# Long convolution and SwiGLU block: even/odd decimated transforms, a folded filter, spectra kept by lane, and shift rows loaded in even partition groups

## The chip, the cores and the metric

The kernel runs on one core of a Trainium2 chip. Times are device microseconds (us) of whole executions. The kernel before takes 399.01 us (median of 4 runs, the profiled one among them, 397.53 to 400.22). "Span" is the length of the one execution that was profiled.

Engine names in the profiles: PE is TensorE (matrix products), PEld its weight load, DVE is VectorE, ACT is ScalarE, POOL is GpSimd, SP is SyncE, which only issues transfers here. "L379" is line 379 of that run's own kernel. The same statement has a slightly different number in different runs.

## The reference, cut to what matters

There are 2048 positions of 640 channels. A short causal filter (4 taps) is applied to `k`, the result is multiplied by `v`, and a causal convolution as long as the sequence follows. Then come a residual, a layer norm and a feed-forward with a gate.

```python
def _A_ref(q, k, v, shift_k, ssm_k, ssm_D):
    k_pad = jnp.pad(k, ((0, 0), (ks - 1, 0), (0, 0)))
    for t in range(ks):                                   # ks = 4
        k_shift = k_shift + k_pad[:, t:t + S, :] * shift_k[:, ks - 1 - t][None, None, :]
    kv = k_shift * v
    ...                                                   # y = causal convolution of kv with ssm_k, by FFT
    y = y + kv * ssm_D[None, None, :]
    return q * y

x = A_q
h = x + _A_ref(_layernorm(x), A_k, A_v, A_shift_k, A_ssm_k, A_ssm_D)
h2 = h + (_silu(_layernorm(h) @ w_gate) * (_layernorm(h) @ w_up)) @ w_down      # 640 -> 1728 -> 640
```

The comparison with the reference is weak on the convolution: the four experiments that spoil it on purpose (a1, a1b, a2, d1) are all recorded as "correct". That the result of the convolution is small beside `x` would explain it, but was not measured. "Correct" says little of the convolution.

## The kernel before

The sequence is cut into 4 blocks of 512 positions. Each block of `kv` is multiplied by a matrix of cosines and sines (`fwd_transform`), each piece of the filter likewise, the spectra are multiplied and added over earlier blocks (`cmac`), and one inverse transform a block gives the convolution. The parts that the change and the argument touch:

```python
    def fwd_transform(src4, dst8):                        # 8 x 4 x 2 matmuls of 320 columns
        for ct in range(NCT):
            ps = psA.tile([P, 2, 512], FP32, name="ps_mm")
            for kt in range(TT_PER_BLK):
                lhsT = WF_t[:, kt, ct * P:(ct + 1) * P]
                for h in range(2):
                    nc.tensor.matmul(ps[:, h, 0:NH], lhsT, src4[:, kt, h * NH:(h + 1) * NH],
                                     start=(kt == 0), stop=(kt == TT_PER_BLK - 1))
            nc.scalar.copy(r3(dst8[:, ct, :]), ps3(ps))

    def cmac(A, X, G, T, first):                          # complex product and sum: 8 operations of 2560
        ...
            nc.vector.tensor_mul(T, Xc, Gc)
            nc.vector.tensor_add(Ac, Ac, T)
            nc.vector.tensor_mul(T, Xs, Gs)
            nc.vector.tensor_sub(Ac, Ac, T)
            ...

    def conv_front_tiles(j, tiles, st):
            ...
            for jj in range(4):                           # k is loaded four times, shifted by a row
                kj = iop.tile([P, D], BF16, name=f"k{jj}")
                if ti == 0 and jj > 0:
                    nc.gpsimd.memset(kj[0:jj, :], 0.0)
                    nc.sync.dma_start(out=kj[jj:P, :], in_=kk[0:P - jj, :])
                else:
                    nc.sync.dma_start(out=kj[:], in_=kk[r0 - jj:r0 - jj + P, :])
            ...

    def ffn_quarter(q):
            ...
                nc.scalar.activation(sig[:csz, :], ps_g[:csz, :], ACT.Sigmoid)
                gc = ffio.tile([P, MBLK], BF16, name="gc")
                nc.scalar.copy(gc[:csz, :], ps_g[:csz, :])
                uc = ffio.tile([P, MBLK], BF16, name="uc")
                nc.scalar.copy(uc[:csz, :], ps_u[:csz, :])
                gs = ffio.tile([P, MBLK], BF16, name="gs")
                nc.vector.tensor_mul(gs[:csz, :], gc[:csz, :], sig[:csz, :])
                nc.vector.tensor_mul(tT[:csz, c, :], gs[:csz, :], uc[:csz, :])
        ...
    for k in range(1, NB):
        conv_front(k)
        pair(k - 1, 1)
        conv_back(k)
        ffn_quarter(k - 1)
        for pp in range(2, NB - (k - 1)):
            pair(k - 1, pp)
```

## Time and profile before

| | before |
|---|---|
| median of the runs | 399.01 us (4 runs, with the profiled one) |
| span of the profiled execution | 397.7 us |
| PE / DVE / ACT busy | 325.7 / 254.7 / 253.8 us |
| matmuls of 320 columns / of 512 columns in the program | 1216 / 560 |
| bytes moved | 68.91 MB |

The page of the kernel before: the span, busy time of each engine with its share and number of instructions, then the busy share in tenths of 40 equal slices, and the chain of work that ended last, by engine.

```profile
span 397.7 us, 5429 instructions
PE 325.7 (82%) x1914; PEld 185.3 (47%) x1936; DVE 254.7 (64%) x413; ACT 253.8 (64%) x447; POOL 68.1 (17%) x95
PE   1038874497899779999779899897998999999995
DVE  1185498500629989999949999983699723233321
DMA  8589847513886996366863716351043332254111
PE 33%; issue 25%; ACT 14%; DMA 13%; DVE 11%; SPq 2%; POOL 2%; POOLq 0%; DVEq 0%; ACTq 0%
```

A digit is about 10 us.

The three steps of a feed-forward chunk that one operation can replace, from the groups by line of the kernel before (columns: line, engine, operation, operands, shapes, count, busy us, mean ns of one, and the idle time before them):

```profile
L362 ACT CAST gc<-ps_g 128x512 bf16<-128x512 f32 x52 | 30.3, 583 | 0.0
L366 DVE TENSOR_TENSOR gs<-gc,sig 128x512 bf16<-128x512 bf16 x52 | 21.6, 419 | 27.6 <-ACT gc L362 27.6
```

### The profile page before, as it was taken

What the parts mean: (1) busy time and instruction counts of PE and PEld (TensorE: products, weight loads), DVE (VectorE), ACT (ScalarE), POOL (GpSimd) and SP (SyncE); (2) the same over time, 40 slices, a digit from 0 to 9 for tenths busy, and PEclk for the clock granted to TensorE, in tenths of its full rate; (3) what the DMA queues carried; (4) which work ended last, traced back from release to release, by engine and by line L of the source; (5) the groups of instructions that cost most, each with busy time, mean ns of one, the idle gap of its engine ahead of it and who ended that gap; (6) DMA issues with size and microseconds to landing.
All of it is one profiled execution on the core that took longest, in us unless ns stands there. A gap on an engine that the chain in (4) does not pass through costs nothing.

```text
span 397.7 us, 5429 instructions
## 1 busy us (share of the span) xinstructions
PE 325.7 (82%) x1914; PEld 185.3 (47%) x1936; DVE 254.7 (64%) x413; ACT 253.8 (64%) x447; POOL 68.1 (17%) x95
## 2 busy tenths in 40 slices
PE   1038874497899779999779899897998999999995
PEld 1025542364567324565354355454534554544463
DVE  1185498500629989999949999983699723233321
ACT  1259607999786636479987539976664697166610
POOL 5000001000000303203102211131131111433121
PEclk9999969589999969999999999989999999999999
DMA  8589847513886996366863716351043332254111
GB/s 249 180 314 357 296 146 242 157 66 109 321 303 259 356 335 218 101 178 220 305 190 101 266 49 199 104 155 56 16 141 106 112 96 77 100 155 142 52 51 49
DMA packets 33610, 68.91 MB, mean 173 GB/s; under 512 B 4213, under 2 KB 25904, under 8 KB 31920
## 3 DMA queue, kind: packets, MB, share of 16 engines
q1 hardware_dynamic: 26800, 45.63, 33.7%
q0 software_dynamic: 6784, 22.94, 18.5%
q8 instruction: 15, 0.25, 0.2%
q14 instruction: 11, 0.09, 0.1%
HBM read 56.77 MB, written 11.80 MB: 172 GB/s over the span
## 4 chain that ended last, share of the span: by engine, by line
PE 33%; issue 25%; ACT 14%; DMA 13%; DVE 11%; SPq 2%; POOL 2%; POOLq 0%; DVEq 0%; ACTq 0%
PE ps_g L356 11%; PE ps_mm L376 7%; PE ps_mm L153 6%; PE ps_u L358 6%; PE ps_mm L303 4%; DMA wu_g<-in_B_w_up_dram 3%; ACT gc L362 3%; ACT xln_blk L139 3%; DMA k_148<-in_A_k_dram 2%; DMA wg_g<-in_B_w_gate_dram 2%; ACT junk L124 2%; SPq L250 2%; ACT sig L360 2%; DMA WF_t<-const_wf 1%; DMA wbig<-in_A_shift_k_dram 1%
## 5 line engine op out<-in xcount | busy, mean ns | idle before, releaser
L356 PE MATMUL ps_g<-hlnT,wg_g 128*128 128x512 bf16 (+1 forms) x268 | 70.9, 386 | 11.1 <-DMA wg_g<-in_B_w_gate_dram 6.1
L153 PEld LDWEIGHTS <-WF_t 128*128 128x128 bf16 x512 | 51.3, 101 | 48.7 <-DMA WF_t<-const_wf 13.8
L358 PE MATMUL ps_u<-hlnT,wu_g 128*128 128x512 bf16 (+1 forms) x270 | 70.3, 384 | 2.0 <-ACT uc L364 1.3
L376 PE MATMUL ps_mm<-wd_sb,tT 128*128 128x320 bf16 x448 | 69.6, 302 | 1.0 <-DVE tT L367 1.0
L360 ACT ACTIVATE sig<-ps_g 128x512 bf16<-128x512 f32 (+1 forms) x56 | 33.4, 597 | 50.0 <-PE ps_g L356 44.5
L376 PEld LDWEIGHTS <-tT 128*128 128x128 bf16 x448 | 41.9, 98 | 25.6 <-issue 7.1
L346 POOL DMA_DIRECT2D wg_g<-in_B_w_gate_dram x28 | 24.4, 873 | 168.9 <-PE ps_g L356 156.2
L153 PE MATMUL ps_mm<-gT,WF_t 128*128 128x320 bf16 x256 | 40.8, 313 | 15.1 <-DMA WF_t<-const_wf 13.5
L356 PEld LDWEIGHTS <-wg_g 128*128 128x128 bf16 (+1 forms) x280 | 27.3, 99 | 47.4 <-issue 14.7
L153 PE MATMUL ps_mm<-kv_blk,WF_t 128*128 128x320 bf16 x256 | 39.0, 307 | 6.9 <-ACT Xcur L155 3.9
L358 PEld LDWEIGHTS <-wu_g 128*128 128x128 bf16 (+1 forms) x280 | 27.5, 99 | 34.6 <-issue 3.7
L366 DVE TENSOR_TENSOR gs<-gc,sig 128x512 bf16<-128x512 bf16 (+1 forms) x56 | 23.2, 419 | 30.3 <-ACT gc L362 30.3
L364 ACT CAST uc<-ps_u 128x512 bf16<-128x512 f32 (+1 forms) x56 | 32.8, 586 | 10.8 <-DVE tT L367 3.3
L303 PEld LDWEIGHTS <-WI_t 128*128 128x128 bf16 x256 | 25.8, 102 | 17.5 <-issue 5.3
L362 ACT CAST gc<-ps_g 128x512 bf16<-128x512 f32 (+1 forms) x56 | 32.6, 582 | 0.0
L348 POOL DMA_DIRECT2D wu_g<-in_B_w_up_dram x28 | 24.4, 871 | 34.1 <-PE ps_u L358 21.5
L367 DVE TENSOR_TENSOR tT<-gs,uc 128x512 bf16<-128x512 bf16 (+1 forms) x56 | 23.2, 419 | 7.3 <-ACT uc L364 7.0
L155 ACT CAST Xcur<-ps_mm 128x640 bf16<-128x640 f32 x32 | 21.7, 693 | 9.0 <-PE ps_mm L153 9.0
L124 ACT ACTIVATE junk<-h_t,zero_t 128x640 bf16<-128x640 bf16 x16 | 13.2, 828 | 21.8 <-DVE h_t L313 21.5
L261 DVE TENSOR_TENSOR kv_blk<-kv_blk,ktmp 128x640 bf16<-128x640 bf16 x48 | 23.4, 487 | 0.8
L124 ACT ACTIVATE junk<-x_t,zero_t 128x640 bf16<-128x640 bf16 x16 | 13.3, 831 | 13.0 <-DMA x_t<-in_A_q_dram 12.7
L382 POOL DMA_DIRECT2D out_dram<-o_t x16 | 8.8, 553 | 65.4 <-DVE o_t L381 52.0
(256 smaller groups left out, 412.7 us busy)
## 6 DMA issues: line engine op xcount, KB each, us to landing
wg_g<-in_B_w_gate_dram POOLq DMA_DIRECT2D x24, 320.0 KB, 3.6
wu_g<-in_B_w_up_dram POOLq DMA_DIRECT2D x24, 320.0 KB, 4.2
Hld_129<-hf_dram SPq DMA_DIRECT2D x3, 1280.0 KB, 5.5
Hld_130<-hf_dram SPq DMA_DIRECT2D x3, 1280.0 KB, 9.9
gst<-in_A_ssm_k_dram SPq DMA_DIRECT2D x4, 640.0 KB, 7.7
x_t<-in_A_q_dram SPq DMA_DIRECT2D x16, 160.0 KB, 5.4
v_t<-in_A_v_dram SPq DMA_DIRECT2D x16, 160.0 KB, 3.9
h_dram<-h_t SPq DMA_DIRECT2D x16, 160.0 KB, 2.7
```

Of the source, the lines that this page charges most:

```text
L124: nc.scalar.activation(junk[:], x_tile, ACT.Identity, bias=zero_t[:], scale=1.0, accum_out=mv_out[:, 0:1])
L153: nc.tensor.matmul(ps[:, h, 0:NH], lhsT, src4[:, kt, h * NH:(h + 1) * NH], start=(kt == 0), stop=(kt == TT_PER_BLK - 1))
L261: nc.vector.tensor_add(ks, ks, tmp[:])
L303: nc.tensor.matmul(ps[:, h, 0:NH], lhsT, Acc[:, ct, h * NH:(h + 1) * NH], start=(ct == 0), stop=(ct == NCT - 1))
L346: nc.gpsimd.dma_start(out=wg_g[:, :, 0:ncols], in_=B_w_gate[:, f0:f0 + ncols].rearrange("(kt p) f -> p kt f", p=P))
L348: nc.gpsimd.dma_start(out=wu_g[:, :, 0:ncols], in_=B_w_up[:, f0:f0 + ncols].rearrange("(kt p) f -> p kt f", p=P))
L356: nc.tensor.matmul(ps_g[:csz, :], wg_g[:, kt, off:off + csz], hlnT[:, kt, :], start=(kt == 0), stop=(kt == 4))
L358: nc.tensor.matmul(ps_u[:csz, :], wu_g[:, kt, off:off + csz], hlnT[:, kt, :], start=(kt == 0), stop=(kt == 4))
L360: nc.scalar.activation(sig[:csz, :], ps_g[:csz, :], ACT.Sigmoid)
L362: nc.scalar.copy(gc[:csz, :], ps_g[:csz, :])
L364: nc.scalar.copy(uc[:csz, :], ps_u[:csz, :])
L376: nc.tensor.matmul(ps_o[:, h, 0:NH], lhsT, wd_sb[:csz, c, h * NH:(h + 1) * NH], start=(c == 0), stop=(c == NFCH - 1))
```

## The change

The intent is to do less matrix work. The odd-frequency transform of 512 samples is split by the parity of the position (decimated), so that half of the products serve two frequencies. The filter is folded about its middle before its transform. Complex products become three real ones, on "lanes" S, D and E (sequences of 2 x 640 values a partition, S being made from the sum of D and E), two halves each. Spectra of earlier blocks and of the filter go to DRAM lane by lane and come back when they are needed. Positions are laid out so that partition p holds the four rows 4p to 4p+3, and one transfer of seven rows a partition gives all four taps. In block 0 partition 0 has no earlier rows, so 127 partitions are left to load. The last clause of the title is what the change does about them: it loads groups of 112, 8, 4, 2 and 1 partitions. SiLU is taken straight from PSUM. It is nearly a complete rewrite; the core of the diff, with cuts:

```diff
-    def fwd_transform(src4: bass.AP, dst8: bass.AP):
-        for ct in range(NCT):
-            ...
+    def x_transform(i, kv):
+        t = {}
+        for r in range(2):
+            for n in range(2):
+                dst = spt(f"x{n}{r}")
+                for c in range(2):
+                    ps = ps_mm()
+                    for a in range(2):
+                        s = 2 * a + r
+                        for h in range(2):
+                            nc.tensor.matmul(ps[:, h, 0:NH], cs_t[:, s, n, c * P:(c + 1) * P],
+                                             kv[:, s, h * NH:(h + 1) * NH], start=(a == 0), stop=(a == 1))
+                    evac(dst[:, c, :], ps, i == 0 and r == 1 and c == 1)
+                t[n, r] = dst
+        ...                                  # six sums and differences give lanes S, D, E
-                kj = iop.tile([P, D], BF16, name=f"k{jj}")
-                ...
+    def load_k(i):
+        kt = wk.tile([P, NS + 3, D], BF16, name="krun", bufs=1)
+        if i == 0:
+            nc.vector.memset(kt[0:1, 0:3, :], 0.0)
+            nc.scalar.dma_start(out=kt[0:1, 3:7, :], in_=kk[0:NS, :].rearrange("(o r) d -> o r d", o=1))
+            lo = P
+            while lo > 1:
+                hi, lo = lo, 16 if lo == P else lo // 2
+                (nc.sync if hi == P else nc.scalar).dma_start(
+                    out=flat(kt[lo:hi, :, :]),
+                    in_=bass.AP(tensor=kk.tensor, offset=kk.offset + (NS * lo - 3) * D, ap=[[NS * D, hi - lo], [1, 7 * D]]))
+        else:
+            nc.sync.dma_start(out=flat(kt[:]), in_=rows(kk, i, -3, 7))
+        return kt
...
+                for le in LANES:
+                    a = None
+                    for j in range(i):
+                        hl = load_lane(HD[i - j], le)
+                        xl = Xp[le] if j == i - 1 else load_lane(XD[j], le)
+                        nc.vector.tensor_mul(xl[:], xl[:], hl[:])
+                        if a is None:
+                            a = xl
+                        else:
+                            nc.vector.tensor_add(a[:], a[:], xl[:])
+                    acc[le] = a
...
+    def back(i, acc, xn):
+        ...                                  # inverse transform, h, its statistics
+        mean2, rs2 = ln_stats(h, (1, 3) if i == 0 else ())
+        hlnT = wk.tile([P, NDC, MBLK], BF16, name="hlnT", bufs=1)
+        hn = wkt("hn")
+        for a in range(2):
+            pt = psM.tile([P, 2, 1024], BF16, name="ps_tr", tag="ps_mm")
+            for r in range(2):
+                s = 2 * a + r
+                ln_apply(hn, h, mean2, rs2, s)
+                for kt in range(NDC):
+                    nc.tensor.transpose(pt[:, r, kt * P:(kt + 1) * P], hn[:, s, kt * P:(kt + 1) * P], ident[:])
+                nc.scalar.copy(...)
+        return h, hlnT
...
-                nc.scalar.activation(sig[:csz, :], ps_g[:csz, :], ACT.Sigmoid)
-                ...
+                    nc.scalar.activation(sg[0:np_, :], pss[0][0:np_, :], ACT.Silu)
+                    nc.scalar.copy(uc[0:np_, :], pss[-1][up_lo:up_lo + np_, :])
+                    nc.vector.tensor_mul(tT[0:np_, c, :], sg[0:np_, :], uc[0:np_, :])
...
+    for i in range(1, NB):
+        with at(CONV[i]):                    # at() sets the priority that orders each engine's queue
+            ...
+            nxt = back(i, acc, x_norm(i))
+        ffn(i - 1, *state)
+        state = nxt
```

## The prediction

> **What bounds the kernel now.** The page's first part gives PE 325.7 us (82%), DVE 254.7 (64%), ACT 253.8 (64%) of a 397.7 us span. By stage (busy time in 20 us windows) there are three regimes. To about 144 us the first block and the filter spectra are made; the chain of waits there passes through DMA (WF_t, 13.8 us of weight-load wait), PSUM evictions of ACT and transforms. From 120 to 260 us DVE is nearly full (18.9 to 19.7 of 20 us in most windows) as PE is, with interleaved feed-forward and convolution. From 320 us only the last feed-forward is left, on PE.
>
> **Costs, from groups kept apart by form.** A 320-column matmul costs 0.141 us in a dense run (56 in 7.92 us in the chain), a 512-column one 0.227 us (ten in 2.27 us). PSUM evictions on ACT take 0.69 us, statistics passes 0.83 and 0.74. A bf16 tensor_tensor takes 0.419 us for 512, 0.488 for 640, 1.482 for 2560 elements: 0.15 + 0.52 per thousand, so an estimated 0.82 for 1280. [...]
>
> **Removed.** 320-column matmuls fall from 1216 to 848, 512-column ones from 560 to 540: about 57 us of dense PE time (317 to 260). ACT loses one of three evictions in each feed-forward chunk, normalizations (32 x 0.91) and nearly all table loads (14 x 1.28), gains output evictions: about 206 us. The k rows are loaded once, not four times, q once.
>
> **Added.** The combinations of lanes on DVE: butterflies before and after, three real products for each complex one (6 of 1280 instead of 4 of 2560), folds. My count of the new instructions gives 267 us, slightly more than now. Spilled spectra: about 78 lane transfers of 0.33 MB; total bytes an estimated 62 MB (now 68.9).
>
> **On the critical path.** The new kernel becomes DVE-bound in the middle. My stage sum: block 0 ready by about 70 us; three filter pieces, bound by evictions, to 100-108 us (feed-forward starts here, now 144); then DVE works without much pause from the filter combination to the last inverse's inputs: 180 us of work, 190 with gaps between instructions, so to about 290. PE has slack there, waiting for lane products and for second-norm statistics before the transposes (8-13 us each, they stand ahead of the down projection). Then inverse, statistics, transposes (20 us), a dense down projection (16), last feed-forward (31 + 16), store (5): about 375 us. Overlaps that I count as serial pull it down a little: 368. So only about half of the PE saving arrives.
>
> **Predicted:** 368 us, 8 in 10 between 340 and 393. Chances: faster 0.86, same 0.11, slower 0.03.
>
> **What would show it.** PE busy near 265-285 us; DVE busy 255-285 and above 85% in windows from 105 to 290 us, and nearly idle in the last 60; ACT near 205; feed-forward matmuls starting near 100 us; PE idle before inverse transforms put down to DVE, before transposes to DVE/ACT; tensor_tensor of 1280 at 0.82 us; last 60 us dense PE.
>
> **What would make it wrong.** DVE forms slower than assumed (reversed operand in the folds, broadcast weights in the shift, interleaved rows): [...]. Lane loads on the one in-order SP queue blocking weight loads behind a buffer that is not free; stores sharing the engines (the spectra h3 share a buffer with the feed-forward's tT). A slow start (many small loads in block 0) would add 10 us. Faster than 340 would mean that DVE's work overlaps startup or its instructions are cheaper than costed.

A cost for the new tensor_scalar operations is a term of the 267 us counted for DVE, and so of the stage sum, which came to about 375 us and, less the overlaps, to the 368 us predicted. What is said of the one in-order SP queue, the trace of before shows: an issue held that queue for 6.31 us from 5.96 us on, and the next one came at 12.31 us. That stores share engines with loads is read from the page of before, which counts its two large DMA queues against the same 16 engines (33.7% and 18.5% of their span).

## More of the kernel before

From 80 us on PE is 90% busy (286.0 of 317 us). More than half of its idle time (40.3 of 72 us) lies in the first 80 us, where the first block has little to overlap with. Three of PE's waits there (TensorE's timeline of the kernel before; columns: start, length, engine, line, operation, operands, and in brackets the idle time before it with what ended it):

```profile
25.92 9.02 PE L153 MATMUL ps_mm<-gT,WF_t 128*128 128x320 bf16 x48 [13.53 <-DMA WF_t<-const_wf]
52.63 11.47 PE L303 MATMUL ps_mm<-Hld_130,WI_t 128*128 128x320 bf16 x64 [4.41 <-DVE Hld_130 L164]
72.56 1.53 PE L335 MATMUL ps_tr<-ident,hln_t 128*128 128x128 bf16 x10 [8.46 <-ACT hln_t L139]
```

## The result, and the profile after

| | before | after |
|---|---|---|
| median, range | 399.01 us, 397.53 to 400.22 | 368.61 us, 367.69 to 370.26 |
| span of the profiled execution | 397.7 us | 368.5 us |
| PE / DVE / ACT busy | 325.7 / 254.7 / 253.8 us | 276.9 / 248.7 / 190.8 us |
| bytes moved | 68.91 MB | 62.44 MB |

The ratio is 0.9239, with a 95% interval of 0.9205 to 0.9273.

The same lines of the page of the changed kernel:

```profile
span 368.5 us, 4361 instructions
PE 276.9 (75%) x1548; PEld 151.1 (41%) x1548; DVE 248.7 (67%) x408; ACT 190.8 (52%) x340; POOL 30.8 (8%) x50
PE   2490704386697997239999892999999579999992
DVE  2129899697299999889679998997898320111100
DMA  7990770023389999960509999922253500154000
DVE 33%; PE 22%; issue 20%; ACT 11%; DMA 10%; POOL 2%; ACTq 0%; POOLq 0%; SPq 0%; DVEq 0%
```

PE has 48.8 us less to do (325.7 - 276.9), and the kernel is 30.4 us shorter. DVE now leads the chain, and its row stands at 6 to 9 tenths from the 12th slice to the 31st (about 101 to 286 us). PE's row has holes: at the start, near 150 us and near 225 and 290 us. TensorE's timeline of the changed kernel names the largest:

```profile
13.89 2.29 PE L248 MATMUL ps_tr<-ident,gf 128*128 128x128 bf16 x20 [7.88 <-DMA ident<-const_ident]
39.04 6.98 PE L300 MATMUL ps_mm<-kv,cs_t 128*128 128x320 bf16 x28 [11.39 <-DVE kv L286]
60.33 4.42 PE L379 MATMUL ps_mm<-accS,ci_t 128*128 128x320 bf16 x16 [13.33 <-DVE accS L366]
143.72 4.02 PE L379 MATMUL ps_mm<-xS,ci_t 128*128 128x320 bf16 x16 [2.52 <-DVE xS L366]
162.96 2.90 PE L395 MATMUL ps_tr<-ident,hn 128*128 128x128 bf16 x20 [13.01 <-DVE hn L350]
165.93 17.06 PE L444 MATMUL ps_mm<-wd_t,tT 128*128 128x320 bf16 x112
229.83 2.90 PE L395 MATMUL ps_tr<-ident,hn 128*128 128x128 bf16 x20 [7.04 <-DVE hn L350]
297.05 2.90 PE L395 MATMUL ps_tr<-ident,hn 128*128 128x128 bf16 x20 [6.67 <-DVE hn L350]
```

Read lines five and six together. PE finished the inverse transform of block 1 about 150 us, then stood still for 13.01 us until the normalized rows `hn` were there for the transposes. Only then did it start 17.06 us of the down projection of block 0, which needs neither `hn` nor anything else of block 1. It stood behind the transposes in PE's queue: they ended at 165.86 us, and it began at 165.93. The busy time by stretch (columns: stretch, its length, busy us and instructions of PE, PEld, DVE, ACT, POOL, PE's granted clock, DMA share, GB/s) shows both engines there:

```profile
100.00:140.00 40.00, 37.49 (x191) 18.58 (x191) 38.75 (x63) 26.06 (x43) 12.94 (x24) 1.00 1.00 327
140.00:160.00 20.00, 7.43 (x38) 4.05 (x36) 18.43 (x32) 11.16 (x23) 0.00 (x0) 0.77 1.06 351
160.00:200.00 40.00, 36.88 (x221) 21.27 (x222) 33.02 (x48) 23.07 (x43) 3.81 (x4) 0.90 0.36 121
```

From 140 to 160 us DVE has 18.43 of 20 us busy, PE 7.43 and the transfers are at their fullest (1.06). Three explanations suggest themselves: DVE binds, the lane transfers bind, or a ring of hand-offs binds, in which no single engine is full. The experiments tell them apart.

### The profile page after: what moved, and what is told of

It is laid out like the page before. It is cut to its first block, busy times and chain, and to the rows that moved or that the text cites. A ratio compares the mean times of both kernels' runs of the same rounds, so it can differ in the third digit from the quotient of the medians. Undisturbed runs are those within 1.5% of the kernel's fastest.

```text
span 368.5 us, 4361 instructions
## 1 busy us (share of the span) xinstructions
PE 276.9 (75%) x1548; PEld 151.1 (41%) x1548; DVE 248.7 (67%) x408; ACT 190.8 (52%) x340; POOL 30.8 (8%) x50
## 2 busy tenths in 40 slices
DMA packets 59321, 62.44 MB, mean 169 GB/s; under 512 B 13793, under 2 KB 48801, under 8 KB 58787
## 4 chain that ended last, share of the span: by engine, by line
DVE 33%; PE 22%; issue 20%; ACT 11%; DMA 10%; POOL 2%; ACTq 0%; POOLq 0%; SPq 0%; DVEq 0%
PE ps_mm L444 9%; PE ps_mm L379 5%; DMA ident<-const_ident 3%; DVE tT L434 3%; PE ps_mm L300 3%; ACT gT L249 2%; DVE tp L534 2%; ACT junk L335 2%; DMA hd<-Mo 2%; ACT junk L336 2%; DMA ldD<-xd 2%; DMA krun<-in_A_k_dram 1%; PE ps_gu L428 1%; POOL rs L346 1%; PE ps_mm L262 1%
## 5 line engine op out<-in xcount | busy, mean ns | idle before, releaser
L428 PE MATMUL ps_gu<-hlnT,wgu 128*128 128x512 bf16 x540 | 120.0, 379 | 1.9 <-ACT sg L432 1.9
L428 PEld LDWEIGHTS <-wgu 128*128 128x128 bf16 x540 | 52.7, 98 | 63.6 <-issue 2.6
L444 PE MATMUL ps_mm<-wd_t,tT 128*128 128x320 bf16 x448 | 67.5, 308 | 0.2
L432 ACT ACTIVATE sg<-ps_gu 128x512 bf16<-128x512 f32 (+1 forms) x56 | 33.5, 598 | 19.5 <-PE ps_gu L428 17.5
L433 ACT CAST uc<-ps_gu 128x512 bf16<-128x512 f32 (+1 forms) x56 | 32.9, 588 | 20.6 <-PE ps_gu L428 20.4
L434 DVE TENSOR_TENSOR tT<-sg,uc 128x512 bf16<-128x512 bf16 (+1 forms) x56 | 23.3, 418 | 27.5 <-ACT uc L433 27.5
L300 PE MATMUL ps_mm<-kv,cs_t 128*128 128x320 bf16 x128 | 23.7, 329 | 12.2 <-DVE kv L286 11.4
L133 ACT CAST x<-ps_mm 128x640 bf16<-128x640 f32 x30 | 20.2, 710 | 18.5 <-PE ps_mm L300 17.7
L262 PE MATMUL ps_mm<-gT,gb_t 128*128 128x320 bf16 x128 | 24.9, 326 | 6.4 <-ACT gT L249 2.6
L285 DVE TENSOR_TENSOR kv<-kv,kt 128x2560 bf16<-128x2560 bf16 (+1 forms) x15 | 18.1, 1221 | 0.2
```

The lines of the kernel that those rows point to most:

```text
L133: nc.scalar.copy(v2(dst), r3(ps))
L262: nc.tensor.matmul(ps[:, h, 0:NH], gb_t[:, tt, n, c * P:(c + 1) * P], gT[:, src, tt, hs], start=(tt == 0), stop=(tt == 1 and not delta))
L285: nc.vector.tensor_add(kv[:, sl, :], kv[:, sl, :], t[:, sl, :])
L300: nc.tensor.matmul(ps[:, h, 0:NH], cs_t[:, s, n, c * P:(c + 1) * P], kv[:, s, h * NH:(h + 1) * NH], start=(a == 0), stop=(a == 1))
L428: nc.tensor.matmul(ps[:], wgu[:, kt, off:off + P], hlnT[:, kt, :], start=(kt == 0), stop=(kt == NDC - 1))
L432: nc.scalar.activation(sg[0:np_, :], pss[0][0:np_, :], ACT.Silu)
```

## The experiments

Twelve kernels were run, each four times (3 rounds and the profiled run). One caution: an edit can also change the order in which the other instructions stand in the engines' queues (a1, a2 and b2 below show it), so a run need not differ from its partner in the named part alone.

| run | what is changed | median (range), us | ratio to before [95%] |
|---|---|---|---|
| a1_dve_less | after, 18 lane sums left out | 366.87 (365.67-367.17) | 0.9189 [0.9151, 0.9226] |
| a1b_dve_more | after, the 18 sums done twice | 377.72 (376.11-379.97) | 0.947 [0.9419, 0.9521] |
| a2_no_lane_loads | after, 48 lane loads gone | 372.03 (369.0-373.29) | 0.9306 [0.9242, 0.937] |
| a3_pe_more | after, extra matmuls in three feed-forwards | 375.97 (375.46-377.26) | 0.9427 [0.9387, 0.9467] |
| a4_rows_odd | after, shift rows of block 0 in one transfer | 397.88 (396.59-398.83) | 0.9974 [0.9927, 1.002] |
| b1_start | after, identity (now from SyncE's queue) and D loaded first | 363.14 (361.81-364.42) | 0.9105 [0.9058, 0.9151] |
| b2_down_first | after, second norm and transposes emitted after the down projection | 355.04 (353.56-356.38) | 0.89 [0.8847, 0.8954] |
| d1_down_first_dve_less | b2 and a1 together | 347.96 (347.61-348.78) | 0.8727 [0.8689, 0.8765] |
| c1_before_silu | before, SiLU from PSUM alone | 389.51 (388.03-389.97) | 0.9761 [0.9736, 0.9786] |
| c2_before_even | before, even partition groups alone | 394.85 (394.32-395.52) | 0.9904 [0.9881, 0.9927] |
| d2_down_first_start | b1 and b2 together | 351.31 (349.53-352.16) | 0.8804 [0.8775, 0.8833] |
| d3_norm_on_act | d2, normalization of x moved to ScalarE | 358.25 (354.94-359.91) | 0.8973 [0.8923, 0.9024] |

The kernel before took 399.46 us in the rounds of a1 to a3, 399.08 us in those of a4, b1, b2 and d1, and 398.8 us in those of c1, c2, d2 and d3. These lie 0.2% apart, so medians are compared across rounds below; the intervals belong to the ratios to before.

### Does DVE bind? Less and more of its work

```diff
# a1_dve_less                                             # a1b_dve_more: the line stands twice
                         else:
-                            nc.vector.tensor_add(a[:], a[:], xl[:])
+                            pass
```

Both compute a wrong convolution. The 18 sums follow each other every 0.735 us, so they are 13.2 us of DVE (18 x 0.735), all of it in the last two blocks' lane chain.

> The 18 adds over spilled lanes (1280 elements each, 0.735 us from start to start in the trace of after) are left out; result wrong on purpose, loads unchanged. Theory 'vector engine binds the middle': 13.2 us of work goes, 9 to 13 us of time go (368.6 to about 356-360). Rival 'lane loads over DMA bind the middle': within 3 us of 368.6. Rival 'tensor engine binds': within 3 us.

> The same 18 adds are done twice; result wrong on purpose. Theory 'vector engine binds the middle': 11 to 15 us longer (380-384). Rivals (lane loads, tensor engine): 0 to 4 us longer.

Measured: taking them out gained 1.7 us (368.61 to 366.87; the intervals of the two ratios overlap, so this is not clear of zero), doubling them cost 9.1 us. The first misses the theory's 9 to 13 us and lies in the rivals' range, the second lies between the two ranges. An engine that alone set the pace would have given about 13 us both ways. The stretch from 140 to 160 us of a1, and two of DVE's operations in it:

```profile
140.00:160.00 20.00, 5.86 (x38) 3.37 (x36) 16.91 (x25) 10.96 (x23) 0.00 (x0) 0.80 1.03 336
155.01 0.82 DVE L522 TENSOR_TENSOR ldD<-ldD,ldD 128x1280 bf16<-128x1280 bf16 x1 [0.99 <-DMA ldD<-xd]
157.54 0.82 DVE L522 TENSOR_TENSOR ldE<-ldE,ldE 128x1280 bf16<-128x1280 bf16 x1 [0.88 <-DMA ldE<-xd]
```

PE's hole is no smaller (5.86 us busy, before 7.43), although the first of the sums are gone from DVE there. In their place DVE now waits four times for a lane that is still being loaded, 3.12 us together, and small operations of block 1's second norm stand behind these in its queue; PE's wait before the transposes grew from 13.01 to 15.20 us. In the last block the inverse transform does start 6.0 us earlier (274.31, not 280.28), but 45 gate and up matmuls of block 2 then still stand behind it in PE's queue, where the changed kernel has 25. So DVE is close to binding, since more of its work costs at once, but it does not bind alone: where its work goes, loads and PE take its place. From 105 to 290 us the trace of the changed kernel has DVE 168.09 of 185 us busy, 91%, the highest of the engines. The run decides against reading that as a promise: 13.2 us less of that engine's work were worth 1.7 us.

### Do the lane transfers bind?

```diff
# a2_no_lane_loads
-                        hl = load_lane(HD[i - j], le)
-                        xl = Xp[le] if j == i - 1 else load_lane(XD[j], le)
-                        nc.vector.tensor_mul(xl[:], xl[:], hl[:])
+                        xl = Xp[le] if j == i - 1 else spt(f"ld{le[0]}{le[1]}")
+                        nc.vector.tensor_mul(xl[:], Xp[le][:], Xp[le][:])
```

Wrong too: it multiplies what is on the chip already.

> The 48 loads of spilled lanes (15.7 MB) are gone, the products read resident lanes instead; result wrong on purpose, same number of vector instructions. Theory 'vector engine binds': 0 to 6 us shorter, from the few waits of products for loads. Rival 'lane loads bind': 12 us or more shorter.

Measured: 372.03 us, 3.4 us more, not less, which neither the theory nor the rival expected (the intervals of the two ratios just overlap). The stretch of the fullest transfers, and PE's wait before the inverse transform of block 1:

```profile
140.00:160.00 20.00, 7.17 (x35) 3.91 (x33) 19.92 (x29) 9.38 (x20) 0.00 (x0) 0.75 0.36 115
145.78 4.41 PE L379 MATMUL ps_mm<-xS,ci_t 128*128 128x320 bf16 x16 [5.19 <-DVE xS L366]
```

The DMA share fell from 1.06 to 0.36, and PE is as idle as before (7.17 us busy). So the lane transfers alone do not limit this kernel; DVE is full there instead (19.92 of 20 us). Together with a1, where DVE waited for lanes once it had less to do, this says that the two limits lie close to each other; a run without the sums and without the loads was not made. The few us lost come with a changed order: with nothing to wait for, products for block 2 moved ahead of the inverse transform's inputs on DVE, and PE waited 5.19 us for these inputs instead of 2.52. That this order is the whole of the 3.4 us was not tested.

### Has PE slack?

```diff
# a3_pe_more
+                        if i < NB - 1:
+                            nc.tensor.matmul(ps[:], wgu[:, 0, off:off + P], hlnT[:, 0, :], start=True, stop=True)
                         for kt in range(NDC):
                             nc.tensor.matmul(ps[:], wgu[:, kt, off:off + P], hlnT[:, kt, :],
                                              start=(kt == 0), stop=(kt == NDC - 1))
```

The result was recorded as correct; the loop behind the extra product still begins with `start=(kt == 0)`.

> One of five gate/up matmuls is issued twice in the first three feed-forward blocks: 81 more of 0.22 us, 17.8 us of tensor engine work in the middle, result right. Theory 'vector engine binds, tensor engine has slack': 0 to 7 us longer. Rival 'tensor engine binds': 15 to 19 us longer.

Measured: 7.4 us more, for an estimated 17.8 us of extra matmuls, just above the theory's 0 to 7. Where the time went, in TensorE's timeline of this run:

```profile
281.38 2.52 PE L379 MATMUL ps_mm<-ldS,ci_t 128*128 128x320 bf16 x16 [0.68 <-DVE ldS L366]
304.68 0.69 PE L395 MATMUL ps_tr<-ident,hn 128*128 128x128 bf16 x5 [0.16 <-ACT hlnT L396]
```

The last inverse transform starts 1.1 us later than in the changed kernel (280.28), so the extra work was until there absorbed or moved behind it; the last transposes then end at 305.4 us, 5.4 us later (299.95). PE has slack in some stretches and none in others. So neither DVE nor PE is the limit alone, and taking work from one of them gains little as long as the other waits in turn.

This led to the theory of a ring: DVE's lane sums, then the inverse transform on PE, then `h` and its statistics on ACT, DVE and POOL, then the transposes on PE with the down projection of the block before behind them, then the next block's forward transform on PE, and DVE again. In that ring the 13.01 us wait and the 17.06 us of down projection are served one after the other, although they are independent.

### The ring: the down projection first

```diff
# b2_down_first
-        hlnT = wk.tile([P, NDC, MBLK], BF16, name="hlnT", bufs=1)
         hn = wkt("hn")
+        return h, hn, mean2, rs2
+
+    def back_t(i, h, hn, mean2, rs2):
+        hlnT = wk.tile([P, NDC, MBLK], BF16, name="hlnT", bufs=1)
         for a in range(2):
             ...                                   # normalize and transpose, as it was
...
-        state = back(0, acc, xln0)
+        state = back_t(0, *back(0, acc, xln0))
...
         ffn(i - 1, *state)
-        state = nxt
+        with at(CONV[i]):
+            state = back_t(i, *nxt)
```

> The down projection of the block before is now emitted ahead of the transposes of the second norm, so that the tensor engine does it while the statistics are made; result right. New theory 'ring of hand-offs': the wait for the statistics (13.0, 7.0 and 6.7 us of idle tensor engine before the transposes) and the down projection (17 us) stand one after the other in the chain of blocks 1 to 3; 12 to 20 us shorter than 368.6 (349-357). Rival 'vector engine binds alone': only the wait of the last block pays, 5 to 7 us shorter.

Measured: 355.04 us, 13.6 us less than the changed kernel, with the same work. TensorE's timeline of this run, at the place of the lines five and six above:

```profile
142.94 2.35 PE L379 MATMUL ps_mm<-xS,ci_t 128*128 128x320 bf16 x16 [2.42 <-DVE xS L366]
147.69 13.02 PE L447 MATMUL ps_mm<-wd_t,tT 128*128 128x320 bf16 x90
161.95 0.45 PE L398 MATMUL ps_tr<-ident,hn 128*128 128x128 bf16 x5 [1.24 <-DVE hn L350]
162.24 0.98 PE L447 MATMUL ps_mm<-wd_t,tT 128*128 128x320 bf16 x6
140.00:160.00 20.00, 17.34 (x121) 11.07 (x120) 20.00 (x34) 11.72 (x26) 0.60 (x2) 1.00 1.07 361
```

The down projection now runs from 147.69 us, in the time that was idle; the wait before the transposes is 1.24 us instead of 13.01, and the stretch from 140 to 160 us has PE 17.34 us busy (it was 7.43). The waits of blocks 2 and 3 (7.04 and 6.67 us) shrank to 1.12 us and to nothing, but a wait of 12.76 us before the last inverse transform appeared, so that 13.6 us were gained and not the 26.7 us of the three waits. Nothing was removed from any engine. This shows that the order of two independent pieces cost 13.6 us. The edit also emits the normalizations on DVE and the copies on ACT later; their part was not separated from that of PE's queue.

### With the ring cut, is DVE's work worth more?

d1 has both edits, b2 and a1, and is wrong like a1.

> The same, and the 18 adds left out (wrong on purpose). Ring theory: with the hand-off gone the vector engine does bind, so the adds now cost what they take: 9 to 13 us shorter than the run with the down projection first alone, against 1.7 us in the kernel after. Rival (vector engine never bound): within 3 us of it.

Measured: 347.96 us, 7.1 us less than b2 alone. The same 18 sums were worth 1.7 us with the transposes in the way. The rival (they stay hidden) is out; the theory's own figure was too high. PE's wait before the last inverse transform, in b2 and then in d1, shows where they now count:

```profile
277.62 3.97 PE L379 MATMUL ps_mm<-ldS,ci_t 128*128 128x320 bf16 x16 [12.76 <-DVE ldS L366]
270.90 4.26 PE L379 MATMUL ps_mm<-ldS,ci_t 128*128 128x320 bf16 x16 [6.39 <-DVE ldS L366]
```

DVE has become the nearer limit, but not the only one: about half of the 13.2 us arrives.

### The start: two small loads first

```diff
# b1_start
-        wrow = wk.tile([1, D, 4], BF16, name="wrow", tag="hlnT", bufs=1)
-        nc.scalar.dma_start(out=wrow[:], in_=A_shift_k.rearrange("(o d) j -> o d j", o=1))
         D5 = cpool.tile([P, NDC, 1], BF16, name="D5")
         with nc.allow_non_contiguous_dma(reason="one column of 640 values"):
             nc.scalar.dma_start(out=D5[:], in_=A_ssm_D.rearrange("(c p o) -> p c o", p=P, o=1))
         ident = cpool.tile([P, P], BF16, name="ident")
-        nc.scalar.dma_start(out=ident[:], in_=id_h.ap())
+        nc.sync.dma_start(out=ident[:], in_=id_h.ap())
+        wrow = wk.tile([1, D, 4], BF16, name="wrow", tag="hlnT", bufs=1)
+        nc.scalar.dma_start(out=wrow[:], in_=A_shift_k.rearrange("(o d) j -> o d j", o=1))
```

> The identity is the first load of its queue, the diagonal vector ahead of the shift weights; result right. If the start is a serial part, the first transposes begin near 8 us rather than at 13.9 and the whole is 4 to 6 us shorter; if something else of the start binds (the last shift rows, which land at 28.5 us), 0 to 2 us.

Measured: 363.14 us, 5.5 us less. TensorE's timeline of this run at the two places of the first two lines of after:

```profile
7.53 2.32 PE L248 MATMUL ps_tr<-ident,gf 128*128 128x128 bf16 x20 [0.20 <-DVE gf L229]
31.85 4.84 PE L300 MATMUL ps_mm<-kv,cs_t 128*128 128x320 bf16 x20 [5.63 <-DVE kv L286]
```

The first transposes start at 7.53 us, not 13.89; the wait of 7.88 us for an identity of 32 KB is gone (in the changed kernel it landed 12.0 us after its issue, and the 640 values of D 10.3 us after theirs); the forward transform of block 0 starts at 31.85 us, not 39.04. Of 7.2 us won there, 5.5 reach the end. The second of these gains has a step between. The small groups of shift rows are issued from ACT's queue, in turn with its evictions. The last of these issues, in the changed kernel and then in this run:

```profile
23.33 0.23 ACTq L163 DMA_DIRECT2D krun<-in_A_k_dram  x1
14.26 0.23 ACTq L163 DMA_DIRECT2D krun<-in_A_k_dram  x1
```

DVE's first tap, which needs these rows, began at 28.51 us and, in this run, at 21.32. By this order of events the late identity delayed the transposes, these ACT's evictions, and these the issue of the last shift rows; that is read from the timelines, not tested. The move of the identity to SyncE's queue and the new order on ACT's queue were not tried apart.

### The last clause undone: 127 partitions in one transfer

```diff
# a4_rows_odd
-            lo = P
-            while lo > 1:
-
-                hi, lo = lo, 16 if lo == P else lo // 2
-                (nc.sync if hi == P else nc.scalar).dma_start(
-                    out=flat(kt[lo:hi, :, :]),
-                    in_=bass.AP(tensor=kk.tensor, offset=kk.offset + (NS * lo - 3) * D, ap=[[NS * D, hi - lo], [1, 7 * D]]))
+            lo, hi = 1, P
+            nc.sync.dma_start(
+                out=flat(kt[lo:hi, :, :]),
+                in_=bass.AP(tensor=kk.tensor, offset=kk.offset + (NS * lo - 3) * D, ap=[[NS * D, hi - lo], [1, 7 * D]]))
```

The same bytes, the same result, one transfer in place of five.

> One part undone: the shift rows of block 0 are loaded by one transfer of 127 partitions instead of groups of 112, 8, 4, 2, 1. The trace of before has transfers of 126 and 125 partitions that held the issuing queue for 6.3 us and landed 8.1 us after their issue; if that comes back here, 2 to 6 us longer. If it is only the number of partitions' rows that counts, within 2 us, or shorter, for the last group now lands only at 28.5 us.

Measured: 397.88 us, 29.3 us more than the changed kernel, and a ratio to before of 0.9974: the whole gain of the rewrite is gone. The expectation (some us) was far off. Lines of this run, first from TensorE's timeline, then from SyncE's queue (an issue of a transfer, with the time that the queue was held by it), and the stretch from 10 to 20 us; the last line is that stretch of the changed kernel:

```profile
66.14 6.88 PE L297 MATMUL ps_mm<-kv,cs_t 128*128 128x320 bf16 x32 [41.78 <-DVE kv L283]
2.24 22.97 SPq L169 DMA_DIRECT2D vt<-in_A_v_dram  x1
10.00:20.00 10.00, 8.70 (x41) 4.36 (x42) 0.00 (x0) 4.43 (x5) 0.00 (x0) 1.00 0.06 26
```

```profile
10.00:20.00 10.00, 5.42 (x30) 2.88 (x31) 2.18 (x6) 3.05 (x3) 0.00 (x0) 1.00 1.04 339
```

The DMA share is a mean over 16 engines. 0.06 is as much as one of them would give if it alone were busy (1/16 = 0.0625); which engines moved the rows was not looked at. 26 GB/s went through in that stretch, where the split version has 339 GB/s. At that rate 1.14 MB (127 x 7 x 640 x 2 bytes) take an estimated 44 us. DVE's first tap indeed began at 55.62 us, after 47.70 us of waiting for `krun`; in the changed kernel it began at 28.5 us. The next issue on the same queue was held for 22.97 us, so other loads of the start came late too: `ci_t` was issued at 46.75 us, in the changed kernel at 12.05.

Size alone is not the cause. In this same run the shift rows of blocks 1 to 3, seven rows of 128 partitions and 1120 KB each, landed 5.4 us after issue where the trace gives it (in the changed kernel 4.9 to 8.2 us). Why 127 partitions in one transfer go so slowly, no run shows, and no other count was tried in its place; that the split into 112, 8, 4, 2 and 1 removes it was measured.

### One part alone on the kernel before: SiLU

```diff
# c1_before_silu
-                nc.scalar.activation(sig[:csz, :], ps_g[:csz, :], ACT.Sigmoid)
-                gc = ffio.tile([P, MBLK], BF16, name="gc")
-                nc.scalar.copy(gc[:csz, :], ps_g[:csz, :])
+                nc.scalar.activation(sig[:csz, :], ps_g[:csz, :], ACT.Silu)
 ...
-                gs = ffio.tile([P, MBLK], BF16, name="gs")
-                nc.vector.tensor_mul(gs[:csz, :], gc[:csz, :], sig[:csz, :])
-                nc.vector.tensor_mul(tT[:csz, c, :], gs[:csz, :], uc[:csz, :])
+                nc.vector.tensor_mul(tT[:csz, c, :], sig[:csz, :], uc[:csz, :])
```

> The kernel before with one part of the change alone: Silu from PSUM in place of Sigmoid, a copy and a product. It takes 56 copies (32.6 us of ScalarE) and 56 products (23.2 us of VectorE) away and leaves the TensorE work as it is. Theory (before is bound by TensorE, 82% busy, and a chunk of the gate and up projections takes TensorE longer than ScalarE): 0 to 8 us less, 391 to 399 us. Rival (ScalarE and VectorE in the projections bind before, so that this part carries a large share of the 30 us): 15 us or more less, under 384 us.

Measured: 389.51 us, 9.3 us less, just outside the theory's range of 0 to 8 and far from the rival's 15. The profile has 32.1 us of ACT and 19.0 us of DVE less, and PE nearly as busy as before (320.6 and 325.7), so most of what was removed was hidden, as the theory said, but less completely than it said. That a chunk takes TensorE longer than ScalarE holds in the trace of before: ten products in 2.27 us where they are dense (1.19 + 1.08), and three passes on ACT of 0.598, 0.583 and 0.587 us, together 1.77 us.

### One part alone on the kernel before: even groups

```diff
# c2_before_even
-                    nc.sync.dma_start(out=kj[jj:P, :], in_=kk[0:P - jj, :])
+                    for lo, hi in ((16, P), (8, 16), (4, 8), (jj, 4)):
+                        (nc.sync if hi == P else nc.scalar).dma_start(out=kj[lo:hi, :], in_=kk[lo - jj:hi - jj, :])
```

> The kernel before with the last clause of the title alone: the three transfers with 127, 126 and 125 partitions of its first tile split into groups of 112, 8, 4 and 3, 2 or 1 partitions. They held the SyncE queue for 6.3 us and let the VectorE wait 6.2 us at the start. Theory (these transfers of 160 KB cost a few us, and the 29 us of the one of 1.1 MB come from its size, so the clause is a cure for the changed kernel's own seven-row transfer): 2 to 6 us less, 393 to 397 us. Rival (the clause is worth some 29 us in any kernel that loads these rows): 370 to 375 us.

Measured: 394.85 us, 3.9 us less; the interval of the ratio (0.9881 to 0.9927) excludes no change, though it is within the 2% that count as the same. SyncE's queue of the kernel before, then of this run, and TensorE's first transform of this run:

```profile
5.96 6.31 SPq L250 DMA_DIRECT2D k_145<-in_A_k_dram  x1
```

```profile
8.60 1.37 SPq L251 DMA_DIRECT2D k<-in_A_k_dram  x3
21.85 8.83 PE L153 MATMUL ps_mm<-gT,WF_t 128*128 128x320 bf16 x48 [7.58 <-DMA WF_t<-const_wf]
```

One issue had held the queue for 6.31 us; the three 112-partition ones that take its place are through in 1.37 us, and the first transform starts at 21.85 instead of 25.92 us. The kernel before had the like in small: one transfer of 127 partitions, about 160 KB, with the one of 126 behind it as the issue that was held. But other loads kept its DMA share near 1 there (1.03 from 6 to 8 us), so the trace does not show this transfer at a low share, as that of a4 does (0.06 from 10 to 20 us). The clause is worth 3.9 us there and 29.3 us in the new kernel, whose one transfer carries seven rows a partition and stands in front of everything else.

### Both gains together, and one step further

d2 has the edits of b1 and b2.

> The changed kernel with both gains together: transposes behind the previous block's down projection in the order of emission (355.0 us alone) and the identity and D loaded first (5.5 us less alone). Theory (the first shortens the middle, the second the start; nothing is shared): 348 to 351 us. Rival (the slack won at the start is eaten by a later wait): 353 to 356 us.

Measured: 351.31 us, the best right version: 17.3 us less than the changed kernel, 12% less than before. It lies 0.3 us above the theory's range and below the rival's: 3.7 of the 5.5 us of the start arrive. What is left shows in TensorE's timeline of this run:

```profile
273.30 4.45 PE L379 MATMUL ps_mm<-ldS,ci_t 128*128 128x320 bf16 x16 [12.76 <-DVE ldS L366]
```

Before the last inverse transform PE waits 12.76 us for DVE's lanes. Behind it in PE's queue stands the down projection of block 2, whose last input DVE finished at 263.7 us, 9.6 us before the wait ends; as it is, that projection fills the wait for block 3's `hn`, which is there at about 290 us. To move a part of it forward, which is the lesson of b2 once more, was not tried. The wait also suggests taking work from DVE, and d3 tried a cheap way:

```diff
# d3_norm_on_act (on top of d2)
         h = wk.tile([P, NS, D], BF16, name="h", bufs=2)
+        if i:
+            nb = small.tile([P, NS], FP32, name="nb")
+            nc.vector.tensor_mul(nb[:], mean, rs[:])
+            nc.vector.tensor_scalar_mul(nb[:], nb[:], -1.0)
+            for s in range(NS):
+                nc.scalar.activation(h[:, s, :], xt[:, s, :], ACT.Identity, bias=nb[:, s:s + 1], scale=rs[:, s:s + 1])
         for r in range(2):
             ...
-                ln_apply(h, xt, mean, rs, s)
+                if i == 0:
+                    ln_apply(h, xt, mean, rs, s)
```

> The same as the run with both gains, and the 12 normalizations of x (640 elements each, 0.44 us, 5.3 us of VectorE in the last three blocks) moved to ScalarE, where each takes 0.9 us, with one small pair of VectorE operations per block added. Theory (with the transposes moved, VectorE work in the lane chain counts at about half its size, 7.1 of 13.2 us): 1 to 3 us less than the run with both gains. Rival (ScalarE evacuates PSUM for the inverse at that place, and its 2.7 us more per block lengthen the chain): same or up to 5 us more.

Measured: 358.25 us, 6.9 us more than d2. The direction was the rival's, the size was above its 5 us, and the place was not the rival's: not at the inverse transform, but earlier, where ACT empties PSUM for the filter spectra. VectorE's and TensorE's timelines of this run:

```profile
95.08 0.83 DVE L502 TENSOR_TENSOR h<-h,Me 128x1280 bf16<-128x1280 bf16 x1 [2.77 <-ACT h L266]
144.42 2.05 PE L385 MATMUL ps_mm<-xS,ci_t 128*128 128x320 bf16 x7 [5.00 <-DVE xS L366]
```

The normalizations of block 1 run on ACT between 93 and 103 us, among those evictions; one takes 1.00 us in this run (mean of the 12). DVE's combination of the filter pieces waits for ACT (2.77 us here, 1.11 in d2), and the inverse transform of block 1 starts at 144.42 us, where d2 has it at 136.90. That is 7.5 us late, as much as the whole loss. ACT is 55% busy over that run; at that place it stands in the chain. How the delay there grows to 7.5 us was not followed step by step. The normalizations of the later blocks alone were not tried.

## Why the prediction was right, and where its reasons were not

The time was right: 368 us were predicted, 368.61 measured. Point by point:

- **PE's saving.** Busy 265 to 285 us predicted, 276.9 measured; bytes 62 MB predicted, 62.44 measured; "only about half of the PE saving arrives": 30.4 of 48.8 us of PE busy time did (62%), or 53% of the 57 us of dense matmul time that the prediction counted. Right.
- **ACT near 205 us.** Measured 190.8. The statistics passes take 0.74 to 0.77 us in the changed kernel; the prediction had 0.83 for one of the two, read from the kernel before. A small miss of size.
- **DVE 255 to 285 us (267 counted).** Measured 248.7, below the range. The duration of an operation of 1280 was right (0.82 predicted, 0.815 to 0.825 measured), and the forms named as a risk were no more than 1% slower than the line drawn from the kernel before: the fold with a reversed operand took 0.82 us, an operation of 1280 on interleaved rows 0.82, and the broadcast taps of 2560 took 1.49, where an operation of 2560 had taken 1.482. What failed is the sum: operations of 1280 that follow each other start every 0.735 us, so a record of 0.82 overlaps the next one. The lengths of all 408 records of DVE add up to 273.6 us, near the 267 that were counted, but they cover only 248.7. Counting start to start would have been better than adding lengths: for these operations lengths overstate the work by 11% (0.816 over 0.735). The cost of the new tensor_scalar operations was taken from no trace; it was too low. Those of 640 elements took 0.44 us, those of 1280 took 0.483. The two differ in form too (two operations with operands read per partition against one with a constant), so they do not give a cost per element.
- **DVE above 85% from 105 to 290 us, nearly idle in the last 60.** It is 168.09 of 185 us (91%) as a whole and falls to 72% from 180 to 200 us; after 310 us it is 8.57 of 58 us. Right in the sum.
- **"DVE then works without much pause ... 180 us of work, 190 with gaps".** The inverse of block 3 started at 280.3 us, with the prediction at about 290. But the reason behind it, a DVE-bound middle, holds only in one direction: 13.2 us more of DVE work cost 9.1 us (a1b), 13.2 us less gave 1.7 us (a1). The middle was a ring of hand-offs in which DVE and PE took turns, and b2 gained 13.6 us by the order of emission alone. This is the step that failed. The prediction even had the piece ("8-13 us each, they stand ahead of the down projection"; measured 13.01, 7.04, 6.67 us) and filed it under slack of PE, where it costs nothing, instead of putting it into the chain.
- **Feed-forward from 100 to 108 us, "now 144".** It starts at 100.82 us, as predicted. But in the kernel before the first gate product stands at 79.29 us, interleaved with the filter transforms; 141.75 us is only where its dense part begins. So the new kernel is 21 us later there, not 40 us earlier. At the start of the first down projection it leads by 6 us (165.93, before 171.9), and at the end of the last one by 31 (361.8, before 393.1).
- **Tail: transposes to end 20 + 16 + 31 + 16 + 5.** The down projection took 16.6 us, the gate and up products 29.3, the last down projection 16.1 from 345.68 us, and the span ends at 368.5. Right.
- **"A slow start (many small loads in block 0) would add 10 us".** Partly so: the last of the small row groups is issued only at 23.33 us and DVE's taps begin at 28.51; the last transposes of block 0 end at 76.8 us, where "about 70" was predicted, and b1 gained 5.5 us at the start. But the one large load that the small ones replace would have cost 29.3 us (a4), the whole gain. The prediction did not see that the last clause of the title decides the result.

So the closeness of the time was luck in part. The last stretch was right: 88 us by its terms, and 88.2 from the last inverse to the end. The middle was put 10 us too long (to 290, measured 280.3), and the 7 us taken off at the end for overlaps that are not named cover most of that. Within the middle two errors of opposite sign meet: DVE's work was put too high (180 us, measured 165.1 from 100.8 to 280.3 us) and its idle time too low (10 us, measured 14.4); the ring was not in the sum as a cost.

## What to carry to other kernels

If PE waits for something in front of independent work, change the order in its queue before taking work from any engine: here the order was worth 13.6 us (b2). A high busy share of another engine does not show that it binds, an experiment that removes some of its work does: DVE was 91% busy from 105 to 290 us, and 13.2 us less of its work gave 1.7 us (a1). For every transfer look at the number of partitions: here one transfer of 127 left the DMA share at 0.06 and 26 GB/s (a4), and groups of 112, 8, 4, 2 and 1 in its place, with 1.04 and 339 GB/s in the same stretch, made the kernel 29.3 us shorter. Look also at when a busy engine's queue gets to issue the small ones: the last went out at 23.33 us from ACT's queue, and at 14.26 in b1. A chain can be shortened at its start by the order and the queue of the loads, so put the small ones that the first instruction needs in front: identity and D first were worth 5.5 us (b1).
